# A scan fused with a gated network on one core: the first block in chunks of 64, outputs in steps, a new order of all steps

## The chip, the core and the metric

The kernel runs on one core of a Trainium2 chip. The time is device microseconds for one execution, and less is better. The core has a matrix engine (TensorE, PE in the profile, with its weight loads shown as PEld), three engines for elementwise work (VectorE or DVE, ScalarE or ACT, GpSimd or POOL) and SyncE (SP), which here only issues transfers (DMAs). Each engine runs its own list of instructions in order, and waits on semaphores for the others.

## What is computed

Two stages. The first is a Mamba-2 scan over 4 batches x 8 heads x 768 positions, with head size 32 and state size 16. With `cum` the running sum of log a in a chunk of 32:

```python
L = np.exp(cum[:, :, :, None] - cum[:, :, None, :]) * causal
y_intra = einsum('bhij,bhjd->bhid', einsum('bhin,bhjn->bhij', Cc, Bc) * L, xc)
y_inter = einsum('bhin,bhnd->bhid', Cc, state) * exp(cum)[..., None]
y[:, :, sl] = y_intra + y_inter
state = exp(sum(la))[..., None, None] * state + sum_j(Bx * exp(cum[-1] - cum[j]))
```

The chunk length is a free choice: any length gives the same y. The second stage takes y as 3072 tokens x 256 features, divides each token by its root mean square (with gains `rms_g`), and computes `(silu(xn @ w_gate) * (xn @ w_val)) @ w_out` with 1536 hidden features, all in float32. The weights arrive as 64-bit floats and are turned into 32-bit ones on the chip.

## The kernel before

**Blocks and pairs.** The tokens are cut into six blocks of 512 (numbers 0 to 5 below), and a block into two pairs, each of two chunks of 128 tokens. The scan of block n+1 is done in between the products of block n; the scan of block 0 has nothing to hide behind and makes up the opening.

**The order.** No scheduler decides. A string `order` (L1269) lists some thousand steps as `block:step.numbers`, and the loop at L1437 calls the function of each (from `first_kinds` for block 0, `kinds` for the rest). So every engine's list, and each DMA queue's, is written out by hand. A number after a slash (`0:g.0.1/1`) names the slot of PSUM (two banks) that the step takes.

**The scan of a pair.** `mask` (L457, matmuls L460) writes a causal mask to PSUM, and `sums` (L464; L474, L481) adds differences of running sums of logarithms, taken from a `row` of three bfloat16 parts that `parts` makes on DVE (L397 to L403) out of `r` (L388). `exp` (L486) makes L of it on ACT. `turn` (L540) turns B and C, `T` and its relatives copy them out (L544 to L580) and `scale` (L525) multiplies by decays. `g` (L592, L599) is C times B, `L` (L632, L638) the product with the decay. `A` (`additions`, L664) and `S` (`states`, L671; DVE L678 and L688) make the states. `y` sums the part within a chunk (left operand x, right L) and the part between chunks (left S, right T). All these matmuls are tiled: 32 or 64 rows of the array each, several beside one another. Block 0's two pairs use chunks of 128 (`whole16` as the mask, `first_outputs` L695 with L705 between and L714 within). All later pairs use chunks of 64: g of pairs 2 and 3 by pair (`products_at_once`), from block 2 on by block (`products_of_block`); and `outputs` (L726, matmuls L736) per pair, the between part first, then the within part, then the additions of a later pair.

**The start.** The steps `ident`, `ones`, `never`, `part`, `upto`, `mid` and so on build small constants on DVE and POOL. `idle.7` (L328) is seven bfloat16 matmuls on zeros whose result nobody reads, at the very start; `aT` (L333) turns a, `la0` (L337) clips it, `log` and `log4` (helper L208) take logarithms. `row`, `rowout` and `rowe` (L1147 to L1166) store running sums and their exponentials in DRAM, from which later blocks read them back spread out (`spread`, `dT`).

**The weights.** `fetch.k` (L171) loads one of 18 pieces of the weights; `pow` (two ACT operations), `man` (DVE, L224) and `wt` (DVE, L230) turn it into float32. Pieces come in rotating buffers.

**The network.** `squares` (L769), `yt` (`taken_out`, L791), `ms` (L812), `rs` (`norm_roots`, L824), `rb` and `xn` (`norm_apply`, L842) make the normed tokens. In block 0 the first two tiles of hidden features are multiplied before the norm is known (`early`, L869, matmul L875, normed behind it), and four more plainly (`gate`, L860, matmul L865). Everything else uses Strassen-like products: `P.k.j` (`product_gv`, L933, matmul L951; seven products k of a tile j), `take` (ACT, L957), `C` (DVE, L963), `silug`, `hidg` (L976); `O` (`product_o`, L1060, matmul L1072), `w` (`total_o`, L1103, adds parts of outputs on DVE) and `put` (L1108). Sums of weights and tokens for them are `cw` (L920) and `tx` (L928). `switch` (L1124) closes PSUM slot 0 or 1 and gives its banks to these products.

## Time and profile before

| | |
|---|---|
| median of 3 runs | 389.57 us (389.49 to 389.76) |
| the profiled execution | 389.76 us |
| its span in the trace | 388.0 us, so 1.76 us lie around it |
| busy: PE, DVE, ACT, POOL | 382.5, 277.8, 214.3, 150.1 us |
| DMA | 28.04 MB, 72 GB/s on average |

The profile holds one execution. A row of the timeline reads: start and busy time in us, engine, line of the kernel, operation, output<-inputs by the program's names, shape, how many of them; in brackets the idle time of the engine ahead of it and what ended it. A row for several instructions gives the time from the first one's start to the last one's end or their sum. A row of the waits reads: engine, line that waited, what it waited for, then total us, times and longest us. A row of the windows gives for a stretch its length, then busy time of PE, PEld, DVE, ACT and POOL, the granted clock, the DMA share and GB/s. A row of a group gives total us and mean ns of one instruction, then idle time ahead of them.

### The profile page before, as it was taken

What the parts mean: (1) busy time and instruction counts of PE and PEld (TensorE: products, weight loads), DVE (VectorE), ACT (ScalarE), POOL (GpSimd) and SP (SyncE); (2) the same over time, 40 slices, a digit from 0 to 9 for tenths busy, and PEclk for the clock granted to TensorE, in tenths of its full rate; (3) what the DMA queues carried; (4) which work ended last, traced back from release to release, by engine and by line L of the source; (5) the groups of instructions that cost most, each with busy time, mean ns of one, the idle gap of its engine ahead of it and who ended that gap; (6) DMA issues with size and microseconds to landing.
All of it is one profiled execution on the core that took longest, in us unless ns stands there. A gap on an engine that the chain in (4) does not pass through costs nothing.

```text
span 388.0 us, 9604 instructions
## 1 busy us (share of the span) xinstructions
PE 382.5 (99%) x3805; PEld 330.0 (85%) x3805; DVE 277.8 (72%) x593; ACT 214.3 (55%) x453; POOL 150.1 (39%) x168
## 2 busy tenths in 40 slices
PE   8999999999999999999999999999999999999996
PEld 5676488888888999888899988899888899988995
DVE  6896979876967988669594766868374677454684
ACT  2878677956867272675864244753344571345420
POOL 5022045503693365243568601355611235212231
PEclk9999999999999999999999999999999999999999
DMA  8888988483073404634336112000100001000001
GB/s 91 236 128 233 311 169 179 124 166 30 3 101 87 52 11 96 144 42 100 65 75 85 27 42 42 2 18 19 56 3 2 2 14 48 29 1 0 2 0 56
DMA packets 109940, 28.04 MB, mean 72 GB/s; under 512 B 94824, under 2 KB 107848, under 8 KB 109896
## 3 DMA queue, kind: packets, MB, share of 16 engines
q1 hardware_dynamic: 107816, 27.30, 33.9%
q8 instruction: 30, 0.49, 0.6%
q10 hardware_dynamic: 2080, 0.13, 0.4%
q14 instruction: 14, 0.11, 0.1%
HBM read 23.68 MB, written 3.74 MB: 71 GB/s over the span
## 4 chain that ended last, share of the span: by engine, by line
PE 97%; DVE 1%; ACT 1%; issue 0%; ACTq 0%; DVEq 0%
PE gate L951 29%; PE o L1072 23%; PE val L951 22%; PE o L983 5%; PE gate L865 4%; PE y L736 3%; PE gate L875 2%; PE g L599 2%; PE e L460 1%; PE g L592 1%; PE y L664 1%; PE tp L540 1%; PE e L474 0%; DVE ob L1103 0%; PE idle L328 0%
## 5 line engine op out<-in xcount | busy, mean ns | idle before, releaser
L963 DVE TENSOR_TENSOR c<-val,p 128x512 f32<-128x512 f32 x99 | 67.3, 686 | 49.4 <-PE val L951 35.2
L957 ACT COPY p<-gate 128x512 f32<-128x512 f32 x99 | 56.8, 581 | 61.6 <-PE gate L951 59.3
L951 PE MATMUL gate<-tx,wgv 128*128 128x256 f32 x264 | 65.8, 381 | 0.0
L208 ACT ACTIVATE c<-c 128x256 f32<-128x256 f32 x99 | 40.0, 415 | 39.2 <-DVE c L963 38.9
L976 POOL TENSOR_TENSOR hid<-c 128x256 f32<-128x256 f32 x31 | 23.8, 769 | 89.6 <-ACT c L208 84.9
L951 PEld LDWEIGHTS gate<-tx,wgv 128*128 128x128 f32 x264 | 49.3, 190 | 6.9 <-ACT p L957 0.2
L1103 DVE TENSOR_TENSOR ob<-ob,o 128x128 f32<-128x128 f32 (+1 forms) x90 | 24.2, 297 | 21.7 <-PE o L1072 16.9
L976 DVE TENSOR_TENSOR hid<-c 128x256 f32<-128x256 f32 x68 | 34.0, 513 | 6.7 <-ACT c L208 6.6
L1072 PE MATMUL o<-two,hid 128*128 128x128 f32 x280 | 36.5, 276 | 0.1
L1072 PEld LDWEIGHTS o<-two,hid 128*128 128x128 f32 x280 | 34.5, 192 | 1.1 <-DVE hid L976 0.4
L951 PE MATMUL val<-xn,wgv 128*128 128x256 f32 x132 | 33.7, 381 | 0.0
L951 PE MATMUL val<-tx,sw 128*128 128x256 f32 x132 | 33.5, 380 | 0.0
L951 PE MATMUL val<-xn,sw 128*128 128x256 f32 x132 | 33.3, 381 | 0.0
L951 PE MATMUL gate<-tx,sw 128*128 128x256 f32 x132 | 33.0, 380 | 0.0
L951 PE MATMUL gate<-xn,wgv 128*128 128x256 f32 x132 | 32.7, 380 | 0.0
L493 POOL TENSOR_SCALAR_AFFINE_SELECT L<-L 64x512 f32<-64x512 f32 x32 | 22.8, 713 | 18.1 <-ACT L L208 16.8
L951 PEld LDWEIGHTS val<-xn,wgv 128*128 128x128 f32 x132 | 24.8, 190 | 3.5
L951 PEld LDWEIGHTS val<-tx,sw 128*128 128x128 f32 x132 | 24.9, 190 | 3.4 <-issue 0.2
L951 PEld LDWEIGHTS gate<-tx,sw 128*128 128x128 f32 x132 | 24.8, 190 | 3.4 <-issue 0.2
L951 PEld LDWEIGHTS val<-xn,sw 128*128 128x128 f32 x132 | 24.4, 190 | 3.2 <-issue 0.2
L951 PEld LDWEIGHTS gate<-xn,wgv 128*128 128x128 f32 x132 | 24.4, 190 | 3.1
L208 ACT ACTIVATE u<-gate 128x256 f32<-128x256 f32 (+1 forms) x37 | 14.6, 402 | 18.2 <-PE gate L951 15.3
(202 smaller groups left out, 702.6 us busy)
## 6 DMA issues: line engine op xcount, KB each, us to landing
L<-rowd SPq DMA_DIRECT2D x32, 128.0 KB, 3.3
xr<-in_x_dram SPq DMA_DIRECT2D x24, 128.0 KB, 3.6
out_dram<-ob SPq DMA_DIRECT2D x24, 128.0 KB, 2.4
wr<-in_moe_w_out_dram SPq DMA_DIRECT2D x6, 511.5 KB, 6.3
wr<-in_moe_w_gate_dram SPq DMA_DIRECT2D x5, 511.5 KB, 5.4
wr<-in_moe_w_val_dram SPq DMA_DIRECT2D x5, 511.5 KB
br<-in_B_dram SPq DMA_DIRECT2D x23, 64.0 KB, 2.6
dT<-rowe SPq DMA_DIRECT2D x10, 128.0 KB
```

Source lines behind the costliest of these rows:

```text
L208: nc.scalar.activation(**operands)
L493: nc.gpsimd.affine_select(out=L[r], in_=L[r], pattern=[[0, L.shape[1]], [1, HC]], compare_op=ALU.is_ge, fill=0.0, base=0, channel_multipli ...
L599: nc.tensor.matmul(out=g[u, P * i:P * i + P].rearrange("p (t m) -> p t m", t=2), lhsT=T[r, i, 0, u], rhs=T[r, i, 1:3, u], start=(first and ...
L736: nc.tensor.matmul(out=y[2 * k + u][rows, (2 * n + i) * HC:(2 * n + i + 1) * HC], start=(k, u, rows.start) not in opened, stop=True, skip_ ...
L865: nc.tensor.matmul(out=gv[:, k], lhsT=w[:, t, fs], rhs=xns[0][:, t], start=(t == 0), stop=(t == 1))
L951: nc.tensor.matmul(out=dst[:, half[w]], lhsT=lhsT, rhs=rhs, start=(k in (1, 2, 5) and w == 0), stop=True, skip_group_check=True)
L957: nc.scalar.copy(out=t, in_=Xs[j])
L963: nc.vector.tensor_tensor(out=t, in0=Zs[j], in1=a, op=ALU.add)
L976: engine.tensor_tensor(out=hid[:, 2 * j + c // 10 - 1, c % 10 - 1], in0=u, in1=src[:, half[1]], op=ALU.mult)
L983: nc.tensor.matmul(out=o, lhsT=hid[:, f, k // 2, (k % 2) * P:(k % 2 + 1) * P], rhs=wo[:, f], start=opens, stop=(f == NF - 1), skip_group_c ...
L1072: nc.tensor.matmul(out=Os[blk, b][:, place * P:(place + 1) * P], lhsT=hidden_or_sum(u)[:, g], rhs=rhs, start=(blk, b) not in opened, stop= ...
L1103: nc.vector.tensor_tensor(out=o, in0=o, in1=src, op=ALU.add if what[0] == "+" else ALU.subtract)
```

## The change

- **Chunks of 64 everywhere.** Block 0 is scanned like the others: g by block (`products_of_block`), decays by `decayed_block`, additions of the whole block in one step `AA` (two banks), their products with the mask of heads in two steps `Sn`, and one state per step `S.n`. The code for chunks of 128 is gone.
- **Outputs in steps.** `y` for a block does the part between chunks (in block 0 the first half of the part within), `yw` the part within of one pair, `yb` the part between in block 0, `yn` the additions for the next block. Squares and copies out of PSUM come in four steps each (`sq.0` to `sq.3`, `yt.0` to `yt.3`), and block 0's copy is split between DVE and ACT.
- **Finer steps.** `pow`, `parts`, `rs`, `xn`, `norm`, the constants and `put` (a copy `putc` and the store) are cut so that each instruction can be placed by itself. `middles` is computed on DVE instead of POOL.
- **Buffers.** B and C share five buffers (before three each), x has four (before three); C of the first pair is loaded through ACT's queue.
- **A new order of all steps.** Among them: `idle.7` stands just before block 0's g instead of first; the logarithm `log` stands before `log4`; pieces are fetched in the order 1, 3, 0, 9, 2, 5, 4, 6, 7, 8, 10, 11, 12, 15, 14, 16, 13, 17 (before 0, 1, 2, 3, 4, 7, 5, 8, 9, 6, 11, 10, 12, 13, 15, 17, 14, 16), with other steps' transfers in between; gate.3 comes ahead of gate.2, early.1 ahead of early.0; P.1.3 ahead of y and P.2.3; near the end `w.18` stands earlier on DVE.

The numbers and shapes of the products with weights (L951, L1072, L983, L865, L875) are unchanged. ACT does 4 exponentials of 128x1024 for block 0 and 1 where it did 6, and 24 loads of its tables instead of 22. The tiled passes add up to: within parts 384 of 32x64 (before 320, and 32 more of 32x128), between parts 176 of 64x64 (148, and 12 of 64x128), additions 192 (160), g 192 of 64x128 (160, and 16 of 128x256), by the program's own instructions.

The core of the diff:

```diff
-        br = raw.tile([P, 2, NH, N], FP32, tag="br", name="br")
-        st.setdefault(p, {}).update(B=br)
-        if p < 4:
-            st[p]["C"] = raw.tile([P, 2, NH, N], FP32, tag="cr", name="cr")
-        for i, queue in enumerate(queues):
-            load_chunk(p, i, queue)
+        b, c0 = divmod(2 * p, NC)
+        for name, src, queue in (("B", B, queues[0]), ("C", C, queues[1]))[0:2 if p < 4 else 1]:
+            t = raw.tile([P, 2, NH, N], FP32, tag="br", name="br", bufs=5)
+            st.setdefault(p, {})[name] = t
+            for i in range(2):
+                sl = slice((c0 + i) * P, (c0 + i + 1) * P)
+                queue.dma_start(out=t[:, i], in_=src[b, :, sl, :].rearrange("h s n -> s h n"))
...
-    def power(k):
+    def power(k, stage):
...
-    def from_middle():
-        nc.vector.tensor_copy(out=mid, in_=upto)
-        nc.vector.tensor_scalar_add(mid[0:HC], mid[0:HC], -1.0)
-
-    def from_middles():
-        nc.gpsimd.tensor_copy(out=mid, in_=upto)
-        for r in halves:
+    def from_middles(k):
+        if k == 0:
+            nc.vector.tensor_copy(out=mid, in_=upto)
+        elif k == 3:
+            nc.vector.tensor_scalar(out=mids[:, 1], in0=mid, scalar1=-1.0, scalar2=None,
+                                    op0=ALU.mult)
+        else:
+            r = halves[k - 1]
             half_of = slice(r.start, r.start + HC // 2)
-            nc.gpsimd.tensor_scalar(out=mid[half_of, r], in0=mid[half_of, r], scalar1=-1.0,
-                                    scalar2=None, op0=ALU.add)
-        minus_mid()
-
-    def mask16():
-        for r in halves:
-            nc.vector.tensor_copy(out=never16[r], in_=never[r, r])
-
-    def kinks_of_powers():
-        for k, v in enumerate((-14336.0, -28672.0 * 2.0 ** 19)):
-            nc.vector.memset(kinks[:, k:k + 1], v)
+            nc.vector.tensor_scalar_add(mid[half_of, r], mid[half_of, r], -1.0)
...
+    rooms = {}
+
+    def three_parts(k, stage):
...
+    def first_additions(blk, banks):
+        ps["A", blk] = both = [banks[:, u, 0:256].rearrange(
+            "p (k i t d) -> p k i t d", k=2, i=2, t=2) for u in range(2)]
+        for k in range(2):
+            additions(2 * blk + k, k, both)
...
+    def new_states(blk, u):
+        if blk not in news:
+            news[blk] = ssd.tile([P, 2, 4, 2, D], FP32, tag="A", name="A", bufs=1)
+        nc.vector.tensor_tensor(
+            out=news[blk][:, u], in0=ps["A", blk][u].rearrange("p k i t d -> p (k i) t d"),
+            in1=tmask.unsqueeze(1).unsqueeze(3).to_broadcast([P, 4, 2, D]), op=ALU.mult)
...
-    def first_outputs(p, y):
...
-        if p:
-            inter(0, True)
-        intra(0, p == 0)
-        intra(1, False)
-        inter(1, False)
...
-    def outputs(p, pair, after, n=0):
-
-        first = p - n
-        if n == 0:
-            ps["y pair", p] = pair
-            ps["y", p] = [bank("y2", (P, 512)), pair[:, 0], bank("y3", (P, 512)), pair[:, 1]]
-        y, s, opened = ps["y", first], st[p], set()
-        width = 1 if p < 4 else 2
-
-        def product_y(k, u, i, rows, **operands):
-            nc.tensor.matmul(out=y[2 * k + u][rows, (2 * n + i) * HC:(2 * n + i + 1) * HC],
-                             start=(k, u, rows.start) not in opened, stop=True,
-                             skip_group_check=True, **operands)
-            opened.add((k, u, rows.start))
-
-        for i in range(2):
+    opens = {}
+
+    def outputs(blk, pair):
+        ps["y pair", blk] = pair
+        ps["y", blk] = [bank("y2", (P, 512)), pair[:, 0], bank("y3", (P, 512)), pair[:, 1]]
+        opens[blk] = set()
+        if blk > 0:
+            outputs_between(blk)
+        else:
+            outputs_within(blk, 0)
...
+    def outputs_between(blk):
+        turns = blk > 0
...
+    def outputs_within(blk, i):
+        turns = blk > 0
+        p = 2 * blk + i
+        for j in (2 * i, 2 * i + 1):
...
+    def next_additions(blk):
+        if blk + 1 == NBLK:
+            return
+        y = ps["y", blk]
+        ps["A", blk + 1] = A_ps = [y[u][:, 256:512].rearrange(
+            "p (k i t d) -> p k i t d", k=2, i=2, t=2) for u in range(2)]
+        for k in range(2):
+            additions(2 * blk + 2 + k, k, A_ps)
...
+    def squares(blk, stage):
...
+    def norm_roots(blk, stage):
...
+    def norm_apply(blk, t=0):
```

The order up to the first products with normed tokens, after:

```
0:ident 0:kinks.0 0:mean 0:ones 0:a 0:zeros 0:whole.0 0:upto 0:warm 0:upto2 0:middles.0 0:part 0:whole.2
0:ident16 0:never 0:never16.0 0:part2.0 0:whole.1 0:middles.2 0:never16.1 0:after 0:part2.1 0:bc.0 0:after2
0:middles.1 0:mask.1/0 0:hmask 0:aT 0:tmask 0:eps 0:middles.3 0:part2.2 0:head 0:mask.0/1 0:turn.0 0:la0 0:log
0:log4.0.4 0:log4.6.2 0:Tb.0 0:sel 0:x.1 0:r.0 0:parts.0.0 0:parts.0.1 0:parts.0.2 0:parts.0.3 0:x.0 0:c/2 0:d
0:dx 0:T.0 0:scale.0.1 0:log4.4.2 0:scale.0.0 0:set 0:tok 0:tokout 0:cx 0:ch 0:bc.1 0:scale.1.1 0:fetch.1
0:sums.0 0:exp.0 0:sums.1 0:fetch.3 0:r.1 0:parts.1.0 0:AA.0/2 0:Sn.0.0 0:parts.1.1 0:turn.1 0:Tb.1 0:T.1
0:row.1 0:rowe.1 0:parts.1.2 0:S.0.0 0:kinks.1 0:exp.1 0:mask.3/1 0:scale.1.0 0:cc 0:Sn.0.1 0:idle.7 0:pow.3.0
0:fetch.0 0:gcol 0:fetch.9 0:pow.3.1 0:bc.3 0:fetch.2 0:S.0.1 0:rowout.1 0:parts.1.3 0:S.0.2 0:S.0.3 0:S.0.4
0:S.0.5 0:g.0/2 0:L1.0.3 0:L1.0.2 0:pow.1.0 0:last.0 0:Tl.0 0:sums.3 0:pow.1.1 0:last.1 0:Tl.1 0:pow.0.0
0:exp.3 0:pow.0.1 0:L.0 0:y.0/0 0:man.1 0:S.0.6 0:wt.1 0:yw.0.1 0:yb.0 0:man.3 0:wt.3 0:yta.0.1 0:S.0.7
0:yt.0.0 0:mask.2/1 0:yta.0.3 0:yt.0.2 0:early.1.0/2 0:bc.2 0:dT.2 0:man.0 0:cw.0.0 0:wt.0 0:pow.9.0 0:sq.0.1
0:sq.0.2 0:cw.0.1 0:cwp.0.3 0:man.9 0:sq.0.0 0:sq.0.3 0:sums.2 0:turn.3 0:row.0 0:rowout.0 0:scale.3 0:pow.9.1
0:wt.9 0:exp.2 0:rowe.0 0:early.1.1 0:man.2 0:cw.0.2 0:pow.2.0 0:pow.2.1 1:exps 0:wt.2 0:cwp.1.0 0:fetch.5
0:fetch.4 0:dT.3 0:ms.0 0:Tt.3.0 0:early.0.0/1 0:x.2 0:cw.1.1 0:Tt.3.1 0:rs.0.0 0:rs.0.1 0:norm.1.0 0:xn.0.0
0:xn.0.1 0:tx.0.2 0:silu.1 0:early.0.1 0:norm.0.1 0:turn.2 0:Tt.2.1 0:cwp.1.3 0:txp.0.0 0:txp.0.1 0:txp.0.3
0:Td.2 0:norm.1.1 0:norm.0.0 0:Tt.2.0 0:hid.1 0:pow.5.0 0:pow.5.1 0:man.5 0:silu.0 0:scale.2 0:T.3 0:pow.4.0
0:man.4 0:wt.5 0:hid.0 0:gate.3/0
```

856 lines of the change are left out of this document (397 added, 459 removed).

## The prediction

> **What bounds the kernel now.** First the head of the page: busy time of each engine, and the chain that ended last by engine.
>
> ```profile
> span 388.0 us, 9604 instructions
> ...
> PE 382.5 (99%) x3805; PEld 330.0 (85%) x3805; DVE 277.8 (72%) x593; ACT 214.3 (55%) x453; POOL 150.1 (39%) x168
> ...
> PE 97%; DVE 1%; ACT 1%; issue 0%; ACTq 0%; DVEq 0%
> ```
>
> TensorE (PE) is busy 382.5 of 388.0 us and carries 97% of the chain. So a change pays only by fewer or cheaper PE passes, or by less time in which PE has nothing; any other engine counts only where PE comes to wait for it. The waits of PE come next, then its busy time (second column) in two stretches: from the first product with weights to the first of the Strassen-like products, and from there to 380 us.
>
> ```profile
> PE idle L328 <- DVE warm L354: 1.1, 1, 1.1
> PE y L705 <- DVE S L686: 0.5, 1, 0.5
> PE o L1072 <- DVE ob L1103: 0.4, 1, 0.4
> ```
> ```profile
> 22.57:50.09 27.52, 27.52 (x334) 16.19 (x332) 22.28 (x50) 21.00 (x34) 4.01 (x5) 1.00 0.90 231
> 50.09:380.00 329.91, 329.77 (x3190) 295.64 (x3185) 233.75 (x480) 179.76 (x395) 138.35 (x144) 1.00 0.27 53
> ```
>
> From 22.57 to 380 PE has no hole. There is nothing to win there by faster feeding, and a new hole is lost time. What can move is the opening (0 to 22.57), the few microseconds that PE spends on the small tiled products of the scan, and the 0.4 us wait near the end.
>
> **The change, part 1: the opening.** It is a chain through several engines. Its rows in before:
>
> ```profile
> 0.89 0.17 DVE L354 MEMSET warm<- 128x128 uint32 x1 [0.89 <-PEq L1463]
> ...
> 1.11 1.68 PE L328 MATMUL idle<-warm 128*128 128x256 bf16 x7 [1.11 <-DVE warm L354]
> ...
> 3.60 0.53 PE L333 MATMUL aT<-ident,a_sb 96*128 96x96 f32 x2
> ...
> 4.17 0.49 DVE L337 TENSOR_SCALAR early<-aT 128x192 f32<-128x192 f32 x1 [0.66 <-PE aT L333]
> ...
> 4.69 0.60 ACT L208 ACTIVATE early_ones<-early 128x128 f32<-128x128 f32 x3 [2.62 <-DVE upto L362]
> ...
> 5.09 1.19 PE L388 MATMUL r_ps<-mids,early_ones 128*128 128x256 f32 x2
> ...
> 6.32 0.42 DVE L397 CAST room<-r_ps 128x256 bf16<-128x256 f32 x1 [0.83 <-PE r_ps L388]
> ...
> 7.70 0.48 DVE L403 SCALAR_TENSOR_TENSOR row<-room,third_part 128x256 bf16<-128x256 bf16 x1
> 9.54 0.40 PE L474 MATMUL e<-row,sel 32*128 32x128 bf16 x8
> ```
>
> Start to start: aT to its clipping 0.57, clipping to logarithms 0.52, to r 0.40, to its first cast 1.23, and 1.86 from there to the end of row. In after, DVE has some 16 small operations (masks, identities, ones) ahead of the first mask of PE, about 0.18 us each, the memset above being one: 0.89 + 16 x 0.18 = 3.7. Two mask passes precede aT, so aT 4.5, clipping 5.1; the order puts the long logarithm ahead of the one that r needs, +0.3: 5.9, r 6.3, cast 7.5, row 9.4. So sums.0 starts at about 9.5, where before starts its own (9.54). Nothing lost so far: before does other work on PE in the same time.
>
> From here DVE leads. After puts one queue of 24 DVE operations between row.0 and the last decayed product L.0, for both pairs at once. Prices by group (in each row: total us, mean ns):
>
> ```profile
> L688 DVE SCALAR_TENSOR_TENSOR S<-S,fcol,A 128x64 f32<-128x64 f32 x36 | 10.6, 296 | 1.0
> L224 DVE TENSOR_SCALAR m<-wr 128x512 int32<-128x512 uint32 x18 | 8.6, 477 | 0.5 <-DMA wr<-in_moe_w_gate_dram 0.3
> L230 DVE TENSOR_TENSOR wgv<-m,e 128x512 int32<-128x512 int32 x12 | 8.5, 714 | 0.5 <-ACT e L208 0.2
> ...
> L632 DVE TENSOR_TENSOR L<-g,L 128x512 f32<-128x512 f32 x8 | 5.3, 681 | 0.7 <-POOL L L493 0.7
> L632 DVE TENSOR_TENSOR L<-g,L 128x1024 f32<-128x1024 f32 x4 | 4.9, 1214 | 0.0
> ...
> L798 DVE TENSOR_SCALAR yt<-y,gcol 128x256 f32<-128x256 f32 x4 | 1.7, 476 | 0.0
> ```
>
> Eleven operations on 128x256 or the like (copies, scalings, the parts of row.1) at 0.42, estimate from the cast: 4.6. Seven states and copies at 0.30: 2.1. One masked turn of 128x512 at 0.69, taken as the L632 row of that size. L.0: 2 x 0.68 + 1.21 = 2.6. Two new states 0.4 each, 0.8. Sum 10.8; overlaps of neighbours (the three parts of a row above start 0.46, 0.51 and 0.41 apart with durations as long) and short waits about cancel. Row 9.4 + 10.8: L.0 ends at 20.2 to 20.8, I take 20.5. PE needs it for y. PE's own work (tiled sums, products, turns, two masks, seven idle passes that now stand here) fills to about 18.5, with a hole of 1.5 before g.0, which waits for Sn.0.1 to free its banks, and 2.0 before y. So after loses 3 to 4 us of PE in its opening, twice what before shows up to 22.57 (22.57 - 20.69 busy). y takes 2.2: 22.7. Then yt waits behind man, wt, man, wt (477 and 714 ns) and two yt (476) on DVE, most of it beside y: done at 24.05. The first early product starts at **24.1, +1.5**. Lower end: if every DVE operation overlaps by 0.07, 23.0; upper: two waits for a DMA or for ACT of 0.5, 25.1.
>
> **Part 2: from early to the Strassen products.** PE's rows in before:
>
> ```profile
> 22.57 3.62 PE L875 MATMUL gate<-yt,wgv 128*128 128x256 f32 x16
> ...
> 27.41 0.48 PE L474 MATMUL e<-row,sel 32*64 32x64 bf16 x33
> ...
> 28.49 0.44 PE L540 MATMUL tp<-ident,br 128*128 128x128 f32 x2
> ...
> 36.48 1.11 PE L599 MATMUL g<-T 32*64 32x128 f32 x32
> 37.52 7.13 PE L865 MATMUL gate<-xn,wgv 128*128 128x512 f32 x16
> 44.58 0.43 PE L664 MATMUL A_ps<-xr,Bd 64*32 64x64 f32 x24
> 44.94 3.70 PE L865 MATMUL gate<-xn,wgv 128*128 128x512 f32 x8
> 48.57 0.49 PE L736 MATMUL y<-T,S 32*64 32x64 f32 x32
> ...
> 50.09 0.70 PE L951 MATMUL val<-xn,wgv 128*128 128x256 f32 x2
> ```
>
> The products with weights are the same in number and shape. What differs before the product P.2.3: sums of one pair instead of two (of 1.08, 27.41 to 28.49): -0.4; the two mask passes of pair 2 stand earlier: -0.5 with their way (0.60 for two, a row below); two passes for the row store are new here: +0.5; g of 64 products instead of 32 (1.04, 36.48 to 37.52) with 64 additions instead of 24 (0.36): +0.8; of y only the between part (0.8 instead of 1.52, 48.57 to 50.09): -0.7; P.1.3 now comes first, four passes of 256 columns (16 passes of 512 take 7.06, 37.52 to 44.58, or 0.22 for 256; 0.215 without the change of shape that the run holds): +0.86; fewer changes between tiled and full products, -0.5 (the gate run of 8 at 44.94 lasts to 48.57, 3.63, of which 0.2 is such a change). Sum 0.1, so 27.52 stays 27.5 and P.2.3 starts at 51.6 against 50.09. P.1.3 being done, that gives **-0.86** back.
>
> Who could be late there: gate.3 needs xn.0 at 33.3 and comes at 33.75; hid.5 is ready at 51.4 for the banks of P.2.3 at 51.55; the pieces of gate.4 and gate.5 are converted at 40 against 43; T of pair 2 at 39.4 against g at 40.6 (estimates by the same prices). Fetching the pieces further apart costs nothing while these hold. They are thin, and the DMA share of this stretch is 0.90. If a piece is 1 us late, PE stands 1 us.
>
> **Part 3: the remaining blocks.** Outputs in steps (between, within, additions) instead of pair by pair change no pass of the large products, and the tiled ones only in their changes of shape.
>
> ```profile
> 61.47 0.46 PE L736 MATMUL y<-T,S 32*64 32x64 f32 x24
> ...
> 63.31 0.92 PE L951 MATMUL gate<-tx,wgv 128*128 128x256 f32 x3
> ```
> ```profile
> 296.57 0.49 PE L736 MATMUL y<-T,S 32*64 32x64 f32 x32
> 296.99 0.86 PE L736 MATMUL y<-L,xr 64*32 64x64 f32 x64
> ```
>
> In a y of before 32 between products take 0.42 until the within products start; by their spacing (8.7 ns a hardware pass) 0.28 of it is work and 0.14 the change of shape. Before pays this twice a block, after runs all of one shape together and pays once or not at all, and joins the additions with ms: I take -0.115 a block, **-0.46** for blocks 2 to 5 (ends 0 and -1.1). For the rest of block 1, before has g of pair 3 (0.8), y of pair 3 (61.47 to 63.31 with its way back, 2.05) and ms (0.55), 3.4; after has 128 within products (1.64) and ms with 64 additions (1.4), 3.04: **-0.38**.
>
> The splits into stages (pow, roots, squares, outputs, put) issue the same operations at other places; ACT, which holds most of them, is busy 55% of the span and hides them. Without that cover each would cost its length once, 0.4 to 0.6. Moving the middles' operations from POOL to DVE is in the 16 small ones. More buffers for B, C and x let their loads start earlier; on SP's queue each load still stands in order, and what stands behind it is rival 3.
>
> **Part 4: the end.**
>
> ```profile
> 381.03 1.16 PE L1072 MATMUL o<-sw,hid 128*128 128x128 f32 x8 [0.38 <-DVE ob L1103]
> ```
>
> The total that this run of passes waits for stands late on DVE in before and early in after, so its 0.38 and the slow first pass behind it go: **-0.45**. Next late is a product ten steps on, at most 0.25.
>
> **Sum:** +1.5 - 0.86 - 0.38 - 0.46 - 0.45 = -0.65. The profiled execution of before took 389.76 (span 388.0 and 1.76 around it), 0.19 over the median 389.57; -0.65 on either gives 389.1 and 388.9. I predict **388.9** against the median.
>
> **The clock.** The seven idle passes at 1.11 take 1.68, 0.24 each for 256 columns; later two mask passes of 512 columns each take 0.60 together with the pipeline's end, about 0.22 each:
>
> ```profile
> 7.68 0.60 PE L460 MATMUL e<-whole,ident 128*128 128x512 bf16 x2
> ```
>
> So per column PE runs at half speed at first and at full speed from about 7 us. After moves the idle passes to just before g.0, starts PE at 3.7 and lets it wait longer. If full speed comes 2.6 us later, like its first pass, some 2 us of half-speed work cost 1 more; if a wait drops it back, the tiled work of up to 6 us could take up to 3 more. The Trainium skill, "TensorE: Matmul & The Clock Gate", section "Part 1: The HAM clock gate (the "warmup" mystery)", says that half speed is the default, lifted after about 3.4 us of sustained work in a free-running window, and back after an idle window of that length. The trace agrees with the first half; no row of before shows a return. By that rule the change is at risk: this is rival 2.
>
> **Rivals.** 1: The opening is no later. If neighbouring DVE operations overlap and L.0 ends at 19.4, early starts at 23.0 and the sum is -1.75: 387.8, down to 386.5 if two changes of shape go per block. For it: the starts of DVE operations lie closer than their durations add up. Against: waits between engines fill what overlap frees.
> 2, slower: **the clock or the DVE queue of the opening.** PE starts 2.6 later and stands twice; from 1.5 us more than in part 1 the kernel is slower than the bound. Half speed in the opening costs 1 to 3: 390.0 to 391.8, likeliest 390.6. For it: idle passes are gone from the start, and after's PE holes are twice as long. Against: the holes are each under 2 us.
> 3, slower: **late pieces.** SP's queue holds the store of rowe.1 behind a wait for ACT ahead of pieces 0, 9 and 2, and rowout.0 ahead of 5 and 4; DMAs are 0.90 busy there. Pieces 1 to 3 us late give 390.4 to 393.
> 4: the long changes of order cancel elsewhere or the steps do not separate as written: within 0.2% of before.
>
> **Chances.** Forecast (387.9 to 389.9) 0.48, of which 0.25 beyond the bound; rival 1 (386.5 to 387.9) 0.17; rival 2 0.19, of which 0.04 within; rival 3 0.13; rival 4 0.03. A measurement tells about 0.2% (0.78 us) from no change: faster 0.42, same 0.30, slower 0.28. Range 386.5 to 392.0: the ends of rivals 1 and 2 and most of 3; the forecast's own is 387.9 to 389.9.
>
> **What would show it.** The first early product at 24.1 (23 to 25.1); PE waiting about 2 us for DVE before the first within product and 1.5 before g; P.2.3 at 51.6; no PE wait from there to the end; no 0.4 wait near the end. Wrong if early starts after 25.5, passes of 512 columns still take 0.43 after 10 us, or a wait for a weight piece or xn.0 shows between 24 and 80 us.

## The result, and the profile after

The changed kernel takes **393.72 us** (median of 6 runs, 391.29 to 395.03) against 389.46 us for the kernel before in the same rounds (388.49 to 389.76): a ratio of **1.0105, 95% interval 1.007 to 1.0141**. It is slower, by about 4 us; 388.9 was predicted, and the range ended at 392.0. The profiled execution of after took 394.13 us with a span of 392.3, that of before 389.76 with 388.0. So the two traces differ by 4.3 us, as the medians do, and what makes the difference can be looked for in them. Below, medians are over all runs of a kernel, while the ratios leave out the runs that took over 1.5% longer than its fastest: 560.92 us of e2's six, 394.45 and 994.16 us of e13's twelve.

First the page of after: span, busy times, the granted clock and the DMA share in 40 slices (of 9.8 us each), and the chain by engine.

```profile
span 392.3 us, 10000 instructions
...
PE 380.2 (97%) x4017; PEld 329.7 (84%) x4017; DVE 269.5 (69%) x584; ACT 216.2 (55%) x447; POOL 144.9 (37%) x161
...
PEclk9999999999999999899999999999999999999999
DMA  8678898856922445673000000000000010100001
...
PE 84%; SPq 4%; DVE 4%; DMA 3%; ACT 3%; issue 1%; POOL 0%; DVEq 0%
```

PE carries 84% of the chain where it carried 97%, and SP's queue, DMA, DVE and ACT now stand in it. One slice of the clock, the 17th (157 to 167 us), shows an 8. The DMA row of before, to set beside it:

```profile
DMA  8888988483073404634336112000100001000001
```

In before the transfers go on to about 242 us, with empty slices from 97 and from 136 us; in after they are done by 186, and no slice before that is empty.

Then the waits of PE. Those of after from 50 us on (before's only one in that part was the 0.38 us near the end, now gone):

```profile
PE o L1004 <- DVE ob L1035: 2.5, 1, 2.5
...
PE ms L745 <- POOL sq L715: 0.5, 1, 0.5
...
PE gate L883 <- DVE xn L778: 0.2, 1, 0.2
```

The windows tell where these lie. Columns: stretch, length, busy time of PE, PEld, DVE, ACT and POOL, clock, DMA share, GB/s. Before:

```profile
150.00:175.00 25.00, 25.00 (x237) 22.19 (x237) 18.22 (x35) 14.56 (x26) 9.11 (x12) 1.00 0.45 93
```

After:

```profile
150.00:175.00 25.00, 22.03 (x244) 19.44 (x248) 15.54 (x44) 14.72 (x31) 16.13 (x19) 0.93 0.64 104
175.00:310.00 135.00, 135.00 (x1282) 121.89 (x1269) 85.91 (x172) 68.89 (x152) 46.95 (x46) 1.00 0.07 20
```

In this execution the loss is in 25 us: there PE stands 25.00 - 22.03 = 2.97 us, and its clock is 0.93, worth 0.07 x 25 = 1.75 us (as much as 3.5 us at half clock). Together 4.7 us. Everything else is small beside it; from 175 to 310 us PE has no hole at all.

The timeline of that place, all engines of after (SPq is SP issuing transfers; in brackets the idle time ahead and what ended it):

```profile
152.03 3.09 SPq L134 DMA_DIRECT2D squares<-in_B_dram  x4
...
156.16 0.45 DVE L526 STREAM_TRANSPOSE T<-squares 128x256 f32<-128x256 f32 x1 [4.35 <-DMA squares<-in_B_dram]
...
157.86 0.45 DVE L1035 TENSOR_TENSOR ob<-ob,o 128x128 f32<-128x128 f32 x2
...
158.36 1.16 PE L1004 MATMUL o<-two,hid 128*128 128x128 f32 x8 [2.50 <-DVE ob L1035]
...
159.35 1.72 PE L883 MATMUL gate<-tx,sw 128*128 128x256 f32 x4
...
160.87 1.91 PE L883 MATMUL gate<-xn,wgv 128*128 128x256 f32 x4
```

Read it from the bottom. Four gate passes take 1.72 and four more 1.91 us, 0.43 each or more, where four of the same shape take 1.03 at full clock (e13's row below): PE runs at half clock. Ahead of them it stood 2.50 us, for totals of the output (step `w`, L1035) on DVE. These were ready to run, but stood in DVE's list behind a turn (L526, step `3:T.0.0`: the first pair's B of block 4), and that turn waited 4.35 us for a load. The load was issued only at 152 to 155 us.

Why so late? SP's queue in after from 116 us on:

```profile
115.98 1.82 SPq L1040 DMA_DIRECT2D out_dram<-ob  x4
121.72 9.06 SPq L134 DMA_DIRECT2D squares<-in_C_dram  x16
130.88 0.59 SPq L548 DMA_DIRECT2D dT<-rowe  x1
...
134.72 3.50 SPq L134 DMA_DIRECT2D squares<-in_B_dram  x4
```

and in before:

```profile
126.71 1.02 SPq L133 DMA_DIRECT2D squares<-in_C_dram  x2
131.51 2.01 SPq L150 DMA_DIRECT2D xr<-in_x_dram  x2
133.56 2.17 SPq L133 DMA_DIRECT2D squares<-in_B_dram  x4
145.58 0.35 SPq L833 DMA_DIRECT2D roots<-r  x1
```

SP issues in order, and a transfer takes it 0.5 to 0.9 us on average (9.06 / 16, 3.50 / 4, 2.17 / 4). Taken one by one (shortest, median and longest in ns), most are close to 0.49 us and a few are three to four times as long:

```profile
L134 SPq DMA_DIRECT2D squares<-in_B_dram x40: 328/487/2013, 58.2 to 170.4; - x40
```

In after SP stands from 117.8 until 121.72. The tile for C's squares has one buffer (`bufs=1`), and DVE turns block 3's C out of it from 120.93 to 121.70; so, by these times, SP waits for that buffer with block 4's. Then it issues end to end (121.72 + 9.06 = 130.78, next at 130.88, and so on to 175). In before it stands idle from 127.7 to 131.5 and from 135.7 to 145.6: it has slack where after has a backlog. The demand came forward with the scan: the product g of blocks 3 and 4 in before and in after:

```profile
148.59 1.21 PE L599 MATMUL g<-T 32*64 32x128 f32 x64
...
199.21 1.21 PE L599 MATMUL g<-T 32*64 32x128 f32 x64
```
```profile
137.36 1.21 PE L574 MATMUL g<-T 32*64 32x128 f32 x64
...
174.17 1.21 PE L574 MATMUL g<-T 32*64 32x128 f32 x64
```

Block 4 is scanned 25 us earlier, and its loads must all pass a queue that at that time also carries what the blocks around it need (block 5's B and rows of L, the outputs). The Trainium skill, "Perfetto Trace Analysis", section "What "DMA-bound" means", counts as one kind of bound that the issuing engine's own track is solid with DMA slices. This trace agrees: SP's track is solid, while the DMA engines are only 0.64 busy in the window above. They are still less busy while SP issues C's squares, at much the same time for each transfer:

```profile
122.00:131.00 9.00, 9.00 (x166) 7.78 (x165) 6.84 (x16) 6.26 (x16) 0.99 (x1) 1.00 0.29 28
```

### The profile page after: what moved, and what is told of

The parts are those of the page before. It is cut to its first block, busy times and chain, and to the rows that moved or that the text cites. A ratio compares the mean times of both kernels' runs of the same rounds, so it can differ in the third digit from the quotient of the medians.

```text
span 392.3 us, 10000 instructions
## 1 busy us (share of the span) xinstructions
PE 380.2 (97%) x4017; PEld 329.7 (84%) x4017; DVE 269.5 (69%) x584; ACT 216.2 (55%) x447; POOL 144.9 (37%) x161
## 4 chain that ended last, share of the span: by engine, by line
PE 84%; SPq 4%; DVE 4%; DMA 3%; ACT 3%; issue 1%; POOL 0%; DVEq 0%
PE gate L883 29%; PE val L883 21%; PE o L1004 20%; PE o L915 5%; PE y L660 2%; PE gate L795 2%; SPq L134 2%; ACT e L203 1%; DMA wr<-in_moe_w_gate_dram 1%; DMA wr<-in_moe_w_val_dram 1%; SPq L121 1%; PE g L574 1%; DMA sq<-roots 1%; ACT sq L203 1%; SPq L487 1%
## 5 line engine op out<-in xcount | busy, mean ns | idle before, releaser
L908 POOL TENSOR_TENSOR hid<-c 128x256 f32<-128x256 f32 x31 | 22.8, 741 | 96.2 <-ACT c L203 96.1
L908 DVE TENSOR_TENSOR hid<-c 128x256 f32<-128x256 f32 x68 | 32.7, 490 | 13.8 <-ACT c L203 13.5
L1004 PE MATMUL o<-two,hid 128*128 128x128 f32 x280 | 37.9, 276 | 2.5 <-DVE ob L1035 2.5
L1035 DVE TENSOR_TENSOR ob<-ob,o 128x128 f32<-128x128 f32 (+1 forms) x90 | 24.5, 297 | 22.8 <-PE o L1004 20.9
L883 PE MATMUL gate<-xn,wgv 128*128 128x256 f32 x132 | 34.2, 390 | 0.2 <-DVE xn L778 0.2
L883 PE MATMUL gate<-tx,sw 128*128 128x256 f32 x132 | 33.8, 387 | 0.0
L978 POOL TENSOR_TENSOR s<-hid 128x512 f32<-128x512 f32 x13 | 17.9, 1373 | 29.5 <-DVE hid L908 22.8
```

Source lines behind the costliest of these rows:

```text
L883: nc.tensor.matmul(out=dst[:, half[w]], lhsT=lhsT, rhs=rhs, start=(k in (1, 2, 5) and w == 0), stop=True, skip_group_check=True)
L908: engine.tensor_tensor(out=hid[:, 2 * j + c // 10 - 1, c % 10 - 1], in0=u, in1=src[:, half[1]], op=ALU.mult)
L978: engine.tensor_tensor(out=hidden_or_sum(o), in0=hidden_or_sum(in0), in1=hidden_or_sum(in1), op=ALU.add if in1[0] == "+" else ALU.subtract)
L1004: nc.tensor.matmul(out=Os[blk, b][:, place * P:(place + 1) * P], lhsT=hidden_or_sum(u)[:, g], rhs=rhs, start=(blk, b) not in opened, stop= ...
L1035: nc.vector.tensor_tensor(out=o, in0=o, in1=src, op=ALU.add if what[0] == "+" else ALU.subtract)
```

## Experiments

The theories. **M**: late loads of SP's queue make one step on DVE wait, PE waits behind it, and the clock falls. **D** is sharper: several readers stand in line, so that behind the first the next one waits. Against them, **K**: the clock or the DVE queue of the opening (rival 2) costs the time; and **N**: the new step functions themselves cost, whatever their order. Each ratio below is against the kernel before in the same rounds.

**e1: one reader later.** In after's order:

```diff
-  2:sq2.0.1 3:T.0.0 1:w.8 ... 1:w.25 2:take.6.0
+  2:sq2.0.1 1:w.8 ... 1:w.25 3:T.0.0 2:take.6.0
```

> After with one step moved: the transpose of block 4's second half of B (3:T.0.0, DVE) stands behind the last total of block 1's outputs (1:w.25) instead of ahead of 1:w.8. Theory M (the late load of the B squares holds DVE's queue, PE waits 2.5 us for a total behind it, and PE's clock drops to half for 8 passes, 1.7 us more): 393.7 - 4.2 = 389.5, between 389.0 and 390.3, no DVE wait of 4 us and a granted clock of 1.00 at 160 us. Rival K (the new opening, with the idle passes late, sets the loss by the clock): unchanged, 393 to 394.5. Rival D (the DMA queue itself is the bound, and the next step that needs a late load stands as long): 392 or more.

Measured: 394.23 us, ratio 1.0126 (1.0099 to 1.0153): no gain. The wait of PE at this place is 0.76 instead of 2.50, and at 160 us PE is 3.8 us ahead of after. It loses this again at once:

```profile
163.22 0.80 DVE L507 TENSOR_TENSOR Bd<-br,d_sb 128x256 f32<-128x256 f32 x1 [3.25 <-DMA br<-in_B_dram]
...
165.85 3.35 PE L883 MATMUL val<-xn,wgv 128*128 128x256 f32 x8 [3.17 <-DVE ob L1035]
```

The next reader in DVE's list (step `3:scale2.1`) waits for its own load, and PE stands 3.17 us, again followed by half clock (0.42 a pass in the row of 8). M with one stall falls; D stands. (The expectation calls `3:T.0.0` the second half of B; it is the B of the first pair.)

**e2: only the clock.** After, with 20 bfloat16 passes on zeros behind `2:yn`, added onto the additions, just ahead of the pass that waits:

```diff
+    def keep(blk, n):
+        for k in range(n):
+            nc.tensor.matmul(out=ps["y", blk][0][:, 256:512], lhsT=warm[:, 0:P], rhs=warm,
+                             start=False, stop=True, skip_group_check=True)
```

> After with 20 bfloat16 passes of zeros behind the additions for block 2 (2:yn), added onto the sums of those additions, so that they change no value; they take about 2.1 us inside the 2.5 us in which PE stands. If the half speed that follows comes from PE's standing: the wait stays about as long or shows as 0.4, the clock stays at 1.00 at 160 us, and the time falls by the 1.7 us of the slow passes to 392.0 (391.5 to 392.5). If the clock falls for another reason: 393.7, unchanged.

Measured: 394.8 us, ratio 1.0136 (1.0113 to 1.0159). In its trace:

```profile
155.72 2.36 PE L704 MATMUL y<-warm 128*128 128x256 bf16 x20
157.91 1.06 PE L1009 MATMUL o<-two,hid 128*128 128x128 f32 x8
158.81 1.03 PE L888 MATMUL gate<-tx,sw 128*128 128x256 f32 x4
```

PE starts the same pass 0.45 earlier than in after, the four gate passes take 1.03, and no slow pass follows: about 1.8 us less at this place. So the half clock came from the stand. The profiled span is 391.0; the median is no lower than after's. In the profiled run, 1.0 us goes elsewhere at about 265 us; of its four runs at 394.03 to 395.49 us, three have a granted clock of 0.991 or 0.996 again, so the clock fell in them too, at a place that no trace shows. The clock's share is shown in one trace, not in the time.

**e3: idle passes first.** After, with `0:idle.7` behind `0:warm`, where before has it.

```diff
-  0:warm 0:upto2 ... 0:Sn.0.1 0:idle.7 0:pow.3.0
+  0:warm 0:idle.7 0:upto2 ... 0:Sn.0.1 0:pow.3.0
```

> After with the seven idle passes moved back to the front, right behind the zeros that they read. Theory M: only the opening moves, 0 to -0.5, so 393.2 to 393.7 (within the scatter of after). Rival K: the opening's half speed is the loss, so at least 2 us faster, 391.7 or less.

Measured: 395.4 us, ratio 1.015 (1.0113 to 1.0186). The first sums come earlier (8.79 against 10.10 us), but PE then waits 1.89 for C of pair 1 and 1.43 before g, and goes to half speed:

```profile
16.40 2.40 PE L574 MATMUL g<-T 32*64 32x128 f32 x64 [1.43 <-DVE A L624]
...
26.52 1.99 PE L807 MATMUL gate<-yt,wgv 128*128 128x256 f32 x8
```

g takes 2.40 where after's takes 1.63, and the first early product starts 3 us later than after's 23.55. The time itself is within what after shows in two measurements (393.72 here, 394.91 in e8). K falls as the main cause: moving the idle passes back doesn't help, the stand of 2.5 us at 160 us is still there, and in after PE is only 0.51 us behind before once the opening is over (the count is below).

**e4 and e7: part 4 alone.** Before, with `5:w.18` earlier on DVE: e4 behind `5:w.12`, e7 behind `5:w.20`.

```diff
-  5:w.20 5:O.12.0 ... 5:w.17 5:w.18 5:w.15
+  5:w.20 5:w.18 5:O.12.0 ... 5:w.17 5:w.15
```

> Before with one step moved: the total w.18 of the last block stands on DVE behind w.12 instead of behind w.17. The prediction's part 4: the wait of 0.38 us at 381 goes, -0.45 against before (389.0); rival: the next product waits instead, 0.0 to -0.2.

> Before with the total w.18 of the last block behind w.20, into a gap of 1.3 us in which DVE waits for PE; the first try put it behind w.12, where the product that it adds was not ready, and held w.8 and w.16 for 0.9 us. The prediction's part 4: the wait of 0.38 us goes, -0.3 to -0.5 (388.7). If the wait only moves to the next total: 0.0 (389.15).

Measured: e4 390.01 us, ratio 1.0022 (1.0013 to 1.0032); e7 389.5 us, ratio 1.0009 (0.9997 to 1.0021). Neither gains. Waits of PE for a total remain near the end, 0.9 in e4 and 0.6 in e7, for other totals or passes. So what the end of after gains isn't the place of `w.18` alone.

**e5: three readers much later.** After, with `3:T.0.0`, `3:T.1.0` and `3:scale2.1` behind `2:P.4.1`.

```diff
-  2:sq2.0.1 3:T.0.0 1:w.8 1:u.14 1:w.22 3:T.1.0 2:subp.3 ... 1:O.14.1 3:scale2.1 3:S.1 ... 2:P.4.1 2:silu.21.1
+  2:sq2.0.1 1:w.8 1:u.14 1:w.22 2:subp.3 ... 1:O.14.1 3:S.1 ... 2:P.4.1 3:T.0.0 3:T.1.0 3:scale2.1 2:silu.21.1
```

> After with three DVE steps that read late loads moved some 14 us later, behind the product P.4.1 of block 3: the transposes of block 4's B (3:T.0.0, 3:T.1.0) and the scaling of block 5's B (3:scale2.1), whose waits of 4.35 us (after) and 3.25 us (first experiment) were seen. The order of all DMAs is unchanged. Theory D (SP's queue has fallen behind by some 10 us, so that loads for the scan of blocks 4 and 5 land late, and whatever DVE step reads one next makes PE wait): the two waits of PE of 2.5 to 3.2 go and the clock stays at 1.00; 389.5 (389.0 to 391.0), unless the next reader of a late load (a subtraction or a decay of block 5) stands, then 391 to 394. Rival P (PE is slowed by something else between 150 and 170 us): 393 to 394.5.

Measured: 397.43 us, ratio 1.0219 (1.02 to 1.0238). PE is 4.57 us ahead of after until about 173 us, so the waits did go. Then:

```profile
176.92 1.04 POOL L493 TENSOR_TENSOR L<-L,tok 128x512 f32<-128x512 f32 x1 [8.39 <-DMA L<-rowd]
...
179.15 2.08 PE L883 MATMUL gate<-tx,sw 128*128 128x256 f32 x4 [5.56 <-ACT p L889]
```

The readers gave their buffers back later, so SP, in order, could not issue the loads behind: it stands from 163.5 to 169.66, when the two turns have just ended on DVE. POOL then stood 8.39 us for a row, and PE 5.56. A reader can be too late as well as too early.

**e6 and e16: another queue.** e6: of block 4's 16 loads of B's squares the last 8 are issued by ScalarE. e16: of its 16 loads of C's squares 8 are issued by POOL, early (their two steps are also moved ahead in the order, which the cut leaves out).

```diff
-                nc.sync.dma_start(
+                (nc.scalar if blk == 4 and k == 0 and h < 2 else nc.sync).dma_start(
```
```diff
-                nc.sync.dma_start(
+                (nc.gpsimd if blk == 4 and k == 1 and h in (0, 3) else nc.sync).dma_start(
```

> After with the last eight of the sixteen loads of block 4's B squares issued on ScalarE's queue instead of SP's; nothing else moves. If SP's queue (its order and the half microsecond that each transfer takes in it) makes the loads late: SP ends 4 us earlier, the transposes wait 0 to 1 us, the scaling of block 5 under 1, and the time falls by 2 to 4 us to 390 to 391.7; ACT pays 8 issues of 0.4 to 0.6 us, which may cost up to 1 us of that. If the DMA engines are the limit (their share is 0.55 to 0.65 there): the loads land as late as before, 393 to 394.5.

> After with eight of the sixteen loads of block 4's C squares issued on POOL's queue, in the 11.8 us in which POOL waits at 118 to 130 us (their step is moved ahead in the order for that); readers and all other transfers stay. If SP's queue is the limit: all that follows on SP comes 3 to 5 us earlier, the transpose 3:T.0.0 waits under 1 us instead of 4.35, and the time falls by 3 to 4.5 us, to 389.5 to 391. If the DMA engines are the limit: the B squares land as late as before (156 us), 393 to 395. POOL may be held over 130 us by its issues, which would show as a wait of PE for the squares' sum at 132 us and cost up to 2.

Measured: e6 400.78 us, ratio 1.0298 (1.0279 to 1.0317); e16 395.06 us, ratio 1.016 (1.0136 to 1.0185). In e6 the loads stood in ACT's own list and left it at 153.7 to 160 us, later than from SP; DVE waited 10.59 and PE 8.7 us. What was left on SP did come earlier: the load of block 5's B that stands behind leaves at 153.07 instead of 158.65. In e16 SP's part of C's squares takes half as long and the first turn waits much less, but a new stand comes first:

```profile
121.42 4.76 POOL L134 DMA_DIRECT2D squares<-in_C_dram  x8 [12.56 <-DVE Bd L507]
```
```profile
121.13 4.16 SPq L134 DMA_DIRECT2D squares<-in_C_dram  x8
...
139.67 0.35 SPq L764 DMA_DIRECT2D roots<-r  x1
...
153.06 3.30 SPq L134 DMA_DIRECT2D squares<-in_B_dram  x4
```
```profile
157.27 0.45 DVE L526 STREAM_TRANSPOSE T<-squares 128x256 f32<-128x256 f32 x1 [0.90 <-DMA squares<-in_B_dram]
```

POOL stood 12.56 us ahead of its first transfer, the work behind it in POOL's list slid by 17 us, and PE, which needs that work by way of DVE and ACT, waited 3.1 us until 131.38. SP, ahead of schedule, then stood before the store of the roots (139.67), so the last loads of B still left at 153. Neither gains time. They say that another queue has an order of its own, and that room in SP's queue is useless behind an instruction that waits. e16 says one thing more: side by side, SP and POOL issued the 16 transfers in 5.05 us (121.13 to 126.18), where SP alone took 9.06 in after. So there the half microsecond lies with the engine that issues, not with the DMA engines that both share.

**e8: after once more**, unchanged, to see its spread.

> After unchanged, beside the other kernels of this call, for its scatter. From its six runs (391.3 to 395.0): median 393 to 394.5, again spread over 3 us or more, since the loads that PE waits for arrive at other times in each run.

Measured: 394.91 us, ratio 1.0164 (1.0145 to 1.0183); in its trace PE waits 3.1 us at the same place, where the first trace has 2.5. Two things in it limit what can be read elsewhere. First, the same kernel gave 1.0105 (1.007 to 1.0141) before, and the two intervals don't meet; so a difference of half a per cent between experiments of different rounds says nothing. Second, the clock. Both traces have the same hole in the opening, 1.04 us ahead of 18.29 in after, here:

```profile
17.79 0.44 PE L562 MATMUL tp<-ident,Cd 128*128 128x128 f32 x2 [1.05 <-DVE L L596]
```

Behind it the clock stays full in after and falls to half in e8. The window from 20 to 22 us, in after and then in e8:

```profile
20.00:22.00 2.00, 1.83 (x140) 1.61 (x141) 1.97 (x5) 2.00 (x4) 0.00 (x0) 1.00 1.09 257
```
```profile
20.00:22.00 2.00, 2.00 (x131) 1.83 (x125) 1.81 (x4) 1.70 (x3) 0.00 (x0) 0.50 1.08 202
```

So whether this hole costs speed differs from run to run of one kernel. In the six runs of after the granted clock over the run is 1.000 once, 0.995 or 0.996 four times and 0.991 once. The run at 1.000 took 393.30 us: in it the loss came without half clock behind a stand, so the division into stand and clock above is that of the profiled run.

**e9 and e10: after's functions in before's order.** e9: after's code and order as far as `0:o.11` (in the middle of block 1); all the rest sorted by the places that the steps have in before. e10: the same, with after's own order again from `5:P.1.0` to the end. An order of a thousand steps can't be shown as a short diff; nothing but the string changes.

> After's code and its order up to the last projection of block 0 (0:o.11, 115 us), then all its remaining steps sorted into the order that before has (steps that before does not know stand where the step stood of which they are parts). So the scan of blocks 3 and 4, which after does at 137 and 174 us against 149 and 199 in before, goes back to before's places. Theory D (the pulled-in scan asks SP's queue for more transfers than it carries in that time, and the late loads make PE wait in one place or another): no wait of PE over 1 us after 115 us, clock 1.00, 389.4 (388.7 to 390.2): before plus 0.5 from the opening, less 0 to 0.5 for changes of shape. Rival N (the new steps themselves, finer and in chunks of a block, cost it wherever they stand): 391 or more.

> As the run before, but from the first product of the last block (5:P.1.0) on in after's order again, with after's end. Theory D: 388.7 (388.0 to 389.7), 0.8 less than the run before, since after's trace gained 0.8 behind the last products of the last block. If the end gains nothing beside another order: as the run before.

Measured: e9 399.16 us, ratio 1.0262 (1.023 to 1.0294); e10 400.59 us, ratio 1.0294 (1.0263 to 1.0325). In e9 the two waits for late loads are gone and the DMA row has empty slices again, but steps that after cuts differently landed badly, and half clock follows the longer of these stands (0.83 on average from 140 to 160 us):

```profile
PE ms L745 <- POOL sq L715: 3.4, 1, 3.4
PE gate L883 <- DVE hid L908: 1.3, 1, 1.3
```

So neither separates N from the order.

**e13: four steps moved.** After, with `3:T.0.0` and `3:T.1.0` behind `1:w.25` (that is, behind the totals that PE needs), `3:scale2.1` behind `3:Td.1`, and the transfer step `3:spread.2.0` ahead of `3:sq2.0.3`, so that no held buffer stands before it in SP's queue. Later than in after, earlier than in e5.

```diff
-  3:T.0.0 1:w.8 1:u.14 1:w.22 3:T.1.0 2:subp.3 ... 1:O.14.1 3:scale2.1 3:S.1
+  1:w.8 1:u.14 1:w.22 2:subp.3 ... 1:O.14.1 3:S.1
...
-  1:w.25 2:take.6.0 3:S.2 3:Td.1 2:P.2.1 ... 3:ex.1 3:sq2.0.3 3:sq2.0.2 3:sq2.0.0 3:spread.2.0 3:subp.2
+  1:w.25 3:T.0.0 3:T.1.0 2:take.6.0 3:S.2 3:Td.1 3:scale2.1 2:P.2.1 ... 3:ex.1 3:spread.2.0 3:sq2.0.3 3:sq2.0.2 3:sq2.0.0 3:subp.2
```

> After with the readers of the three late loads moved only as far as their loads need (3:T.0.0 and 3:T.1.0 behind 1:w.25, 3:scale2.1 behind 3:Td.1, 5 to 10 us instead of 14), and with one transfer that was seen to end a wait (3:spread.2.0, for block 5's decays) taken ahead of the three loads of squares that stand before it in SP's queue. Theory D (late loads through SP's queue and nothing else): the waits of PE between 150 and 180 us are 0 to 1 us in sum, clock 1.00, 389.5 (389.0 to 391.0). If a fourth reader waits for a late load: 392 to 396, with the wait shown there. Rival P (something besides the loads): 393 or more with no wait for a load in the trace.

Measured: **390.37 us, ratio 1.0025 (1.0008 to 1.0042)**. The loss of 1 to 1.6% shrinks to a quarter of a per cent. The same window and the same place in its trace:

```profile
150.00:175.00 25.00, 24.52 (x269) 21.75 (x268) 21.92 (x49) 18.13 (x36) 18.39 (x23) 1.00 0.68 113
```
```profile
155.98 1.16 PE L1004 MATMUL o<-two,hid 128*128 128x128 f32 x8
156.98 1.03 PE L883 MATMUL gate<-tx,sw 128*128 128x256 f32 x4
```

PE stands 0.48 us instead of 2.97, its clock is 1.00, and the pass that started at 158.36 starts at 155.98. DMA is as busy as in after (0.68), and B's last four squares of block 4 leave SP only 1.2 us sooner (at 153.9 instead of 155.1):

```profile
151.85 2.06 SPq L134 DMA_DIRECT2D squares<-in_B_dram  x4
```

So the loads are nearly as late, but nothing that PE needs stands behind their readers. The span is 388.4, 3.9 less than after's. D is confirmed; which of the four steps counts how much, e13 doesn't separate. N is bounded: code, opening and most of the order of after are in e13, and cost 0.08 to 0.42% together. That is what is left after the end of the kernel has given 0.8 us back (by the count of columns below, e13 is 1.26 us behind before at 340 us and 0.45 at the last product). The cure isn't complete: in e13's trace the clock falls to half behind the hole of 1.04 us in the opening, as in e8, and its run of 394.45 us had a granted clock of 0.990.

**e14: e13 with the opening kept warm.** Seven idle passes in front, seven more ahead of g, and B and C of pair 1 loaded earlier, C on ACT's queue.

```diff
-        ps["idle"] = ps.get("idle") or bank("idle", (P, 256))
+        ps["idle"] = bank("idle", (P, 256))
...
-  0:warm 0:upto2 ... 0:bc.0 0:after2 ... 0:ch 0:bc.1 0:scale.1.1
+  0:warm 0:idle.7 0:upto2 ... 0:bc.0 0:bc.1 0:after2 ... 0:ch 0:scale.1.1
...
-        "bc": lambda p: load(p, (nc.sync, nc.scalar if p == 0 else nc.sync)), "sq2": load_squares,
+        "bc": lambda p: load(p, (nc.sync, nc.scalar if p < 2 else nc.sync)), "sq2": load_squares,
```

> As e13_later_fed, with seven more idle passes at the front, the other seven kept before g, and B and C of the second pair loaded right behind those of the first (C on ScalarE's queue), since the third experiment with idle passes in front had its first sums 1.3 us earlier but then waited 1.9 us for that C and fell to half speed. Expected: the first early product 0.5 to 1.3 us earlier than in e13_later_fed and the time less by as much. If x of the first pair is now late, or PE falls to half speed again: equal or up to 2 us slower.

Measured: 392.61 us, ratio 1.0091 (1.0064 to 1.0118), worse than e13 in the same rounds. A wait of 1.12 in y and half speed again; the first early product starts at 26.04 against 23.78 in e13. As in e3, the opening isn't improved by more warming. (An earlier form on e10's order, e11, gave no time: its steps wait for one another in a circle.)

**e15: e13 with its two remaining waits taken out.** `1:txp.2` behind `2:sq.3` on POOL, `1:rb` ahead of `2:spread.3.1` on SP.

```diff
-  1:O.5.0 2:spread.3.1 2:spread.1.1 1:O.11.0 1:rb ... 1:txp.1 1:txp.2 3:dT.1 ... 2:sq.3 1:w.9
+  1:O.5.0 1:rb 2:spread.3.1 2:spread.1.1 1:O.11.0 ... 1:txp.1 3:dT.1 ... 2:sq.3 1:txp.2 1:w.9
```

> As e13_later_fed, with two more steps moved: one sum of tokens on POOL (1:txp.2) behind the sum of squares (2:sq.3) that PE waits for 0.5 us, and the spreading of the roots (1:rb) ahead of two transfers in SP's queue, since PE waits 0.5 us for the tokens that need it. Theory D: both waits go, 390.4 - 1.0 = 389.4 (388.8 to 390.0), so the new order without its late loads equals before. If the opening's scatter is what is left: 390 to 390.8, with both waits gone in the trace.

Measured: 389.93 us, ratio 1.0028 (1.0008 to 1.0048). The waits for sq (0.5) and xn (0.5) are gone; a new one stands in their place, and in the profiled execution the span is 387.7:

```profile
PE y L612 <- DMA xr<-in_x_dram: 0.8, 1, 0.8
```

The ratio is no better than e13's. No version that was run beats the kernel before.

## Why the prediction was wrong

**The opening (part 1) held in its number, in part by luck.** The rows of after:

```profile
23.55 1.99 PE L807 MATMUL gate<-yt,wgv 128*128 128x256 f32 x8
...
51.45 1.13 PE L883 MATMUL val<-xn,wgv 128*128 128x256 f32 x4
```

The first early product starts at 23.55; 24.1 was predicted, with 23 to 25.1 as its ends. DVE's chain came as summed: its row ends at 9.47 (9.4 predicted) and L.0 at 19.96 (20.5). PE's waits did not: 0.42 us before the first within product, and for ACT (2 us for DVE predicted), none before g (1.5 predicted), but 1.04 behind g, at the next turn, and 0.41 at 13.7 us, which the prediction did not have.

**Part 2 and block 1 held.** P.2.3 starts at 51.45, predicted 51.6; the stretch before it took 27.90 us instead of 27.5, so this hit is the sum of a start that was 0.55 early and a stretch that was 0.4 long. With P.1.3 already done, and block 1's rest, the steps added up to 1.5 - 0.86 - 0.38 = +0.26 us. When the columns of the products with weights that PE has done are counted over time in both traces, after stands 0.51 us behind from 82 to 114 us. No weight piece made PE wait: fetching them further apart cost nothing.

**Part 3 failed.** It gave -0.46 us for blocks 2 to 5, with the sentence that each load on SP's queue stands in order and that what stands behind it is rival 3. By the same count of columns, after loses 4.63 us between 115 and 310 us. The failed step is that costing: rows of changes of shape were priced for those blocks, and "who could be late" was asked for the opening and block 0 alone. That the new order brings the scan of blocks 3 and 4 forward was there to be read in it; the loads that come forward with it were not counted in SP's queue. At 0.5 us each they could have been: before shows four such loads in 2.17 us. In the place of -0.46 the trace of after shows 2.50 us of stand, 0.5 and 0.2 in two more waits, and 1.75 us of half clock, 4.9 in all; e13 and the rows above tie the first and the last to the readers' places. What is left over, -0.3, has the sign and the size of the predicted -0.46, but no run measured it by itself.

**Part 4: sign right, reason open.** The end of after gains 0.81 us against before (4.63 + 0.51 = 5.14 behind at 310 us, 4.33 at the last product), predicted 0.45. The row of before's last product, then after's:

```profile
383.81 1.06 PE L1072 MATMUL o<-wo,hid 128*128 128x128 f32 x8
```
```profile
388.55 0.65 PE L1004 MATMUL o<-wo,s 128*128 128x128 f32 x4
```

Their ends are 384.87 and 389.20, 4.33 apart. The reason given, an earlier `w.18`, isn't borne out: e4 and e7 gained nothing in before. What shortens the end is open.

**The rivals.** Rival 3 named the right mechanism, a load late behind SP's queue, at the wrong place: it looked at weight pieces at 25 to 50 us, and gave 0.13. It happened at 122 to 175 us with the scan's loads, and came to 393.72 rather than 390.4 to 393; its price had no clock in it, which is 1.75 us of the profiled run. Rival 2 had the clock, at the opening. In after's trace the hole of 1.04 us at 17.3 us leaves the speed as it is, and in e8, the same kernel, it does not; there the two rows of y behind it take 2.13 and 1.38 us instead of 1.75 and 1.19, about 0.6 us more. So rival 2 came true in that run, at a smaller price than its 1 to 3 us, and the argument against it, holes each under 2 us, does not hold. In both traces the clock fell behind the stand at about 158 us. The prediction cited the Trainium skill, "TensorE: Matmul & The Clock Gate", section "Part 1: The HAM clock gate (the "warmup" mystery)", for a return to half speed after an idle window of about 3.4 us; the trace agrees that it returns, but a stand of 2.50 us sufficed, and in e8 one of 1.05 us. The half speed lasts about as long as the page's window: the clock of 0.93 over 25 us stands for 3.5 us.

**What stays open.** What makes a few transfers take three to four times the usual half microsecond of SP's queue; why the runs of after scatter over 3.7 us, those of before over 1.3 (stretches of half clock account for part: by an estimate from after's granted clocks of 0.991 to 1.000 over 392 us, 0 to 3.5 us are lost to them); whether a second buffer for the squares, which no run tried, would let SP start sooner; and the last 0.25% of e13 and e15. By the columns e15 is 0.65 us ahead of before at 115 us and 0.55 behind at 340 us, so its loss lies in between.

## What to carry to other kernels

A step that is pulled forward brings its loads forward, and they queue: list the transfers of the issuing queue around the new place, multiply by the spacing that the trace shows (here 0.5 us), and set the landing beside the place of the first reader. On an engine with a fixed order, a reader belongs behind everything that the bottleneck waits for soon, yet not so late that its buffer holds the queue: e1, e5 and e13 differ in little else (e13 also moves one transfer). And price a stand of the bottleneck with the clock that may fall behind it; in the profiled run 2.5 us of waiting cost 4.2.

## What the runs showed of the hardware

- The clock fell behind stands of 2.50 us (after), 3.08 us (e8) and 3.17 us (e1), and passes took 0.43 instead of 0.22 us for about 3.5 us. Shorter stands go either way: one of 1.04 to 1.05 us in the opening was followed by half clock in e8 and e13 and not in after, one of 1.59 us near 338 us in e10 was not; in e3 it fell at two of 1.89 and 1.43 close together. In e2, 20 passes on zeros, which filled the wait, kept the clock up in the profiled run.
- Transfers of the scan leave SP at 0.5 to 0.9 us each on average whatever their source (B, C, rows of L), with the DMA engines 0.64 busy and also with 0.29; 16 of them took 9.06 us from SP alone (after) and 5.05 from SP and POOL side by side (e16).
- Eight transfers moved to another engine's queue wait in that engine's own list: in e6, by ACT, the turn that needs them starts at 162.33 us, against 156.16 by SP in after.
